# A clustered-attention and two-stage MoE kernel on one core: a reordered prologue, PSUM operands for some VectorE work, and contiguous early-expert weights

## The chip, the cores and the metric

One core of one Trainium2 chip runs the whole program. Its engines are PE (TensorE: matrix products, with the weight loads listed apart as PEld), DVE (VectorE), ACT (ScalarE), POOL (GpSimd) and SP (SyncE, which here only issues DMAs). Each engine runs its own instructions in order; semaphores tie the engines together. SBUF is the working memory of 128 partitions, PSUM the memory that PE writes to, in eight banks. The metric is the device time of one execution in microseconds, as a median of several runs.

## What is computed

Three stages follow each other: attention with a mask from clusters, an MLP with squared ReLU, and a mixture of eight experts with the best expert for each token.

```python
# attention: batch 2, 8 heads, 768 tokens, 64 wide, 16 centroids per head
q_assign = argmax(normed(q) @ normed(centroids).T, -1); k_assign = the same for k
mask = q_assign[:, :, :, None] == k_assign[:, :, None, :]
scores = where(mask, 0.125 * q @ k.T, -1e9)
x = softmax(scores) @ v                      # -> 1536 tokens x 512
# MLP, 512 -> 2048 -> 512 (w_in, w_out come as float64)
h = maximum(x @ w_in, 0);  x = (s * h * h + b) @ w_out
# experts: 8, 512 -> 1024 -> 512
logits = normed(x) @ normed(expert_emb).T / tau
e = argmax(logits); gate = softmax(logits)[e]
out = gate * (maximum(x @ w1[e], 0) @ w2[e])
```

## The kernel before

**Attention** works on 16 heads (2 batches of 8). Its order is written out by hand: `attention` collects (time, step) pairs in `ops`, sorts them, and pins each step's instructions on all five engines in that order. Head j's steps lie at 12 j plus the offsets in `TIMES`; head j's scores begin at 12 j. The steps of a head are these. `load` issues its q, k and v. `split` makes a rounded copy on ACT and the rest on POOL (on DVE for head 0). `trans` transposes one half of q or k by PE into the PSUM bank "t" (four banks for head 0 alone), copies it by ACT and, after the second half, sends it to the score operand by a DMA from SP. `sims_mm` multiplies with the centroids; `sims_a` to `sims_e` find the nearest one on DVE; `masks` transposes the result into the SBUF tile `ot` and copies it into rows 64 to 95 of the operands `qa` and `ka`: for heads 0 and 1 by ACT and DVE, for heads 2 and 3 by four DMAs of 32 rows, later by DMAs of 16. `M` forms one of twelve score blocks and DVE takes its row maxima; `mneg` and `mrow` turn them into a row that a DMA writes into row 96 of `qa`. `Sx` then forms a score block again with mask and maximum inside (L247, L248) and takes the exponential by ACT (L249). `presum` adds exponentials on POOL, `V` multiplies with v, `sums`, `norm_a` to `norm_c` normalise; the PSUM bank "s2" is shared by `sums`, the maximum row and the first head's maxima. `cst.heat` (`HEAT`) issues matmuls of no use that keep PE busy.

Before, the maxima of head j begin 17.4 steps ahead of its scores. The first head's maxima thus lie among the preparations of heads 1 and 2, each with two warming matmuls, and half of head 1's maxima are formed ahead of head 0's scores. `moe.hooks` adds steps of the later stages to this list: constants (`early`, at `SETUP`), fetches of the float64 weights from ACT's queue (`FETCH`), and their conversion to float32 in nine steps per weight (`CONV`, `conv_steps`) for the first five weights (`NWA`).

**The MLP** (`moe1`) runs three chunks of 512 tokens. A weight block f loads or splits its weights (`wsplit`: ACT rounds, POOL subtracts), forms 12 + 12 matmuls and evacuates. The remaining weights are converted in chunk 0 through PSUM. The routing of chunk c (`route`) runs in pieces, one per weight block of chunk c + 1: `locate` compares the index row `iotas` with each token's rank on DVE, `collect` multiplies the resulting 0/1 matrices, and after chunk 1 `pick` chooses an expert for early work. `eweights` loads its weights by indirect DMAs from POOL; `take` gathers 128 of its tokens. The early expert block (`early_block`, handed out by `fill`) then fills PE while the last chunk is routed and the first rows for the experts are gathered. **The experts** (`experts`, `block`) follow, one after another.

The order in the MLP and the experts is left to the scheduler, but for ACT and DVE in the last routing.

Of the kernel before, what the change touches and what calls it, by code (L numbers as in the profile page):

```python
# [21 lines left out]
P = 128  # L22
# [9 lines left out]
             M=-17.4, mneg=-5.7, mrow=-3.5, V=(5.45, 5.45, 9.45, 9.45, 13.45, 13.45), presum=3.0, norm=(14.5, 25.47, 29.5, 29.5, 29.5))  # L32
ENDS = {14: (14.5, 21.47, 22.4, 23.4, 24.4), 15: (14.5, 14.6, 14.7, 14.8, 14.9)}
WARM = -26
HEAT = ((-41, 7), (-30.5, 6), (-22, 6))
SETUP, FETCH = 6.3, (5.3, 17.3, 29.3)
# [57 lines left out]
def attention(ax, tc, cst, q, k, v, cen, xt, hooks, embed):  # L94
# [110 lines left out]
    def masks(j):  # L205
        i = j % NSET
        ot = w1.tile([P, HS], F32, name="ot", tag="ot")
        nc.vector.transpose(out=ot, in_=si.pop(j))
        for g in range(4):
            da, w = (qa, ka)[g // 2][i], slice(g % 2 * HS, (g % 2 + 1) * HS)  # L210
            if j >= NSET:
                nc.sync.dma_start(out=da[64:64 + NC_, w].bitcast(F32), in_=ot[32 * g:32 * g + NC_])
            elif j > 1:
                nc.sync.dma_start(out=da[64:96, w].bitcast(F32), in_=ot[32 * g:32 * g + 32])
            elif g % 2 == 0:
                nc.scalar.activation(out=da[64:96, w], in_=ot[32 * g:32 * g + 32], func=AF.Copy)
            else:
                nc.vector.tensor_copy(da[64:96, w], ot[32 * g:32 * g + 32])

# [127 lines left out]
    T = TIMES  # L347
    for j in range(NH):
        o = 12 * j
        if j >= 3:  # L350
# [8 lines left out]
        for i, f in enumerate((sims_a, sims_b, sims_c, sims_d, sims_e, masks)):  # L359
            at(o + T["simv"][i], f, j)  # L360
        for r in range(NR):
            for c in range(2):
                at(o + T["M"] + 2 * r + c, M, j, r, c)
                if j == 0:
                    at(o + T["M"] + 2 * r + c, cst.heat, 2, "pv")
        at(o + T["mneg"], mneg, j)
        at(o + T["mrow"] if j else -5.6, mrow, j)
# [13 lines left out]
class Moe:  # L381
# [11 lines left out]
    def hooks(self, ms, mb):  # L393
# [11 lines left out]
        out = [(-27, self.length), (SETUP, early), (-16.6, self.unit), (SETUP + 9, self.project)] + [(t, lambda f=f: fetch(f)) for f, t in enumerate(FETCH)]  # L405
        for f in range(NWA):
            for n, t in enumerate(CONV):
                out.append((36 * f + 16 + t if f < NWA - 1 else 176.2 + n, lambda f=f: next(self.steps(f), None)))
        return out

    def steps(self, f):
        if f not in self.running:
            self.running[f] = self.conv_steps(f)
        return self.running[f]

    def conv_steps(self, f, wide=False):
# [3 lines left out]
        u = [self.ps([P, DM], "cv", "ab"[a]).bitcast(U32) if wide else t[:, a] for a in range(2)]  # L420
        for a in range(2):
            nc.scalar.activation(out=t[:, a].bitcast(F32), in_=r[a][:, :, 1].bitcast(F32), func=AF.Abs)
            yield
        s = t.rearrange("p a (w o) -> p o (a w)", o=2)
        nc.vector.tensor_scalar(out=s.bitcast(F32), in0=s.bitcast(F32), scalar1=CLAMP_LO, scalar2=CLAMP_HI, op0=ALU.max, op1=ALU.min)
        yield
        shift = dict(scalar1=5, scalar2=2, op0=ALU.logical_shift_left, op1=ALU.logical_shift_right)
        if wide:
# [766 lines left out]
```

## Time and profile before

| | us |
|---|---|
| median of 3 runs | 801.79 (798.8 to 803.8) |
| profiled execution | 798.36 |
| its span, first to last instruction | 796.5 |
| PE busy | 758.3 |
| DVE busy | 521.5 |
| ACT busy | 422.7 |
| POOL busy | 347.6 |

Attention fills the span up to about 281 us, the MLP up to about 562, the experts the rest. Busy time is what the profile counts for an engine's instructions; matmuls are pipelined, so a busy PE isn't PE at its peak. The granted clock of PE has two levels, 1.2 and 2.4 GHz, given as 0.5 and 1.0; its mean over the span is 0.983.

### The profile page before, as it was taken

To read this page: it belongs to the slowest core of one execution; us is meant where nothing else is said; L and a number is where in the kernel's file an instruction comes from. 1 tells how busy PE (TensorE), PEld (TensorE's weight loads), DVE (VectorE), ACT (ScalarE), POOL (GpSimd) and SP (SyncE) were. 2 spreads that over 40 slices of the span, in tenths; PEclk is the share of its full clock that TensorE was granted. 3 is DMA by queue.
4 is the path that set the end of the run, shared out by engine and by line. 5 is a ranking of instruction groups with operands and counts; after the bars stand their busy time and mean duration, and the time that the engine had idled before them with its cause. 6 is when DMAs were issued, how large, how long until landed. Compare 5 with 4: busy or idle time off the path is not lost. (4 is left out here: it accounts for less than half of the span.)

```text
span 796.5 us, 12226 instructions
## 1 busy us (share of the span) xinstructions
PE 758.3 (95%) x4193; PEld 574.0 (72%) x4193; DVE 521.5 (65%) x1087; ACT 422.7 (53%) x841; POOL 347.6 (44%) x277
## 2 busy tenths in 40 slices
PE   7699999999999899999999999999999999999994
PEld 3365555555555378888788887778889998989883
DVE  5768889897996889984353542647457445756750
ACT  5266555655644576545445554454447455755650
POOL 2066766776686474454344443545032202230000
PEclk9799999999999999999999999999999999999998
DMA  5145433434321225511000042254133664776600
GB/s 151 41 124 175 113 117 80 137 94 129 87 78 50 73 64 159 177 35 54 1 0 1 27 146 92 80 211 146 56 116 121 222 211 138 243 238 209 217 17 24
DMA packets 75469, 88.72 MB, mean 111 GB/s; under 512 B 7445, under 2 KB 58549, under 8 KB 75008
## 3 DMA queue, kind: packets, MB, share of 16 engines
q1 hardware_dynamic: 66688, 66.52, 27.5%
q0 software_dynamic: 4000, 13.90, 5.4%
q10 hardware_dynamic: 4704, 7.34, 2.8%
q8 instruction: 40, 0.66, 0.3%
q14 instruction: 37, 0.30, 0.1%
HBM read 70.57 MB, written 7.34 MB: 98 GB/s over the span
## 5 line engine op out<-in xcount | busy, mean ns | idle before, releaser
L531 POOL TENSOR_TENSOR wl<-w,wh 128x512 fp32r<-128x512 f32 x96 | 123.0, 1306 | 130.9 <-ACT wh L529 128.3
L249 ACT ACTIVATE pt<-S 128x384 f32<-128x384 f32 x192 | 91.8, 489 | 102.9 <-PE S L248 100.4
L224 DVE TENSOR_REDUCE mx<-M 128x1 f32<-128x384 f32 x192 | 101.9, 552 | 37.7 <-PE M L223 35.7
L260 POOL TENSOR_TENSOR acc<-acc,pt 128x768 f32<-128x768 f32 x61 | 106.3, 1742 | 5.7 <-ACT pt L249 3.3
L552 PE MATMUL hp<-x,wh 128*128 128x512 f32 x384 | 105.9, 397 | 0.2 <-ACT wh L529 0.2
L552 PE MATMUL hp<-x,spare 128*128 128x256 f32 x732 | 96.0, 284 | 2.0 <-PEq L987 1.7
L552 PEld LDWEIGHTS hp<-x,spare 128*128 128x128 f32 x732 | 92.6, 190 | 6.9 <-issue 4.1
L560 PE MATMUL y<-wd,gg 128*128 128x512 f32 x360 | 93.2, 394 | 0.0
L608 DVE SCALAR_TENSOR_TENSOR hp<-hp,sb,t 128x512 f32<-128x512 f32 x48 | 36.3, 757 | 74.1 <-ACT t L607 74.1
L552 PEld LDWEIGHTS hp<-x,wh 128*128 128x128 f32 x384 | 71.2, 189 | 15.1 <-ACT wh L529 0.9
L223 PE MATMUL M<-ka,qa 80*128 80x384 f32 x192 | 78.2, 408 | 3.9 <-DVE mx L224 3.1
L560 PE MATMUL y<-wh,gh 128*128 128x512 f32 x192 | 75.0, 391 | 0.0
L560 PE MATMUL y<-wl,gh 128*128 128x512 f32 x192 | 74.8, 389 | 0.0
L268 PE MATMUL pv<-pt,vn 128*64 128x385 f32 x384 | 74.0, 507 | 0.0
L247 PE MATMUL S<-qa,ka 97*128 97x384 f32 x192 | 71.0, 370 | 2.2 <-ACT pt L249 1.4
L545 DVE TENSOR_TENSOR wd<-w,wd 128x512 fp32r<-128x512 f32 x64 | 43.3, 686 | 44.1 <-ACT wd L544 43.4
L560 PEld LDWEIGHTS y<-wd,gg 128*128 128x128 f32 x360 | 63.8, 189 | 9.9
L1036 POOL DMA_INDIRECT row<-rows,idx x24 | 27.9, 1163 | 93.9 <-PE tp L1048 50.8
L607 ACT ACTIVATE t<-hp 128x512 f32<-128x512 f32 x48 | 28.7, 598 | 71.7 <-PE hp L552 71.7
L248 PE MATMUL S<-qb,kb 128*128 128x384 f32 x192 | 65.5, 341 | 0.0
L223 PEld LDWEIGHTS M<-ka,qa 80*128 80x128 f32 x192 | 36.7, 191 | 38.0 <-DVE su L296 8.1
L560 PE MATMUL y<-wh,gl 128*128 128x512 f32 x192 | 59.1, 389 | 0.0
(269 smaller groups left out, 1361.2 us busy)
## 6 DMA issues: line engine op xcount, KB each, us to landing
w<-in_moe_w_dram SPq DMA_DIRECT2D x128, 256.0 KB
raw<-in_moe_w_in_dram SPq DMA_DIRECT2D x9, 512.0 KB
raw<-in_moe_w_out_dram SPq DMA_DIRECT2D x9, 512.0 KB
raw<-in_moe_w_in_dram ACTq DMA_DIRECT2D x7, 512.0 KB
raw<-in_moe_w_out_dram ACTq DMA_DIRECT2D x7, 512.0 KB
qn<-in_q_dram SPq DMA_DIRECT2D x16, 192.0 KB
kn<-in_k_dram SPq DMA_DIRECT2D x16, 192.0 KB
vn<-in_v_dram SPq DMA_DIRECT2D x16, 192.0 KB
```

Source lines behind the costliest of these rows:

```text
L223: nc.tensor.matmul(pp, qa[i][0:80, r * P:(r + 1) * P], ka[i][0:80, c * HS:(c + 1) * HS])
L224: nc.vector.tensor_reduce(out=mxt[j % 2][:, r, c:c + 1], in_=pp, axis=AX.X, op=ALU.max)
L247: nc.tensor.matmul(pp, ka[i][0:97, t * P:(t + 1) * P], qa[i][0:97, w], start=True, stop=False)
L248: nc.tensor.matmul(pp, kb[i][:, t * P:(t + 1) * P], qb[i][:, w], start=False, stop=True)
L249: exps.setdefault((j, t), []).append(nc.scalar.activation(out=p[:, c, 0:HS], in_=pp, func=AF.Exp, scale=0.125).ins)
L260: eng.tensor_tensor(out=acc[j][-1], in0=acc[j][-1], in1=p[:, :, 0:HS], op=ALU.add)
L268: together(tc, [lambda c=c: nc.tensor.matmul(pv_t[j][c * 64:c * 64 + 64, :], io_t["v", j][:, t, :], p[:, c, :], start=t == 0, stop=t == NR ...
L531: eng.tensor_tensor(out=wl[:, a], in0=w[:, a], in1=wh[:, a].bitcast(F32), op=ALU.subtract)
L545: eng.tensor_tensor(out=t[:, 1], in0=w[:, a], in1=t[:, 0].bitcast(F32), op=ALU.subtract)
L552: self.nc.tensor.matmul(hp, a[:, k * P:(k + 1) * P], b(k), start=n == 0, stop=n == 3 * KD - 1)
L560: self.nc.tensor.matmul(y[i], (gl if n == 2 else gh)[:, s], wl if n == 1 else wh, start=first and n == 0, stop=last and n == 2)
L608: nc.vector.scalar_tensor_tensor(out=hp, in0=hp, scalar=sb[:, 0:1], in1=t, op0=ALU.mult, op1=ALU.mult)
```

## The change

The times of the attention steps get a table for heads 0 to 4 (`FIRST`) in place of `TIMES`. Head 0's maxima come straight behind its masks, 0.4 steps apart and with one warming matmul each, its maximum row right behind them; the warming groups ahead and behind are 16 and 10 long. Heads 2 and 3 are transposed and given their masks later, behind the first scores of head 0; the maxima of heads 1, 2 and 3 come later and closer together. Heads 0 to 2 transpose their masks inside PSUM (`ot` is the PSUM tile itself) and copy them from there, half by DVE in `masks`, half by ACT in the new step `copies`; head 2 issues no mask DMAs any more. The constants move ahead of the first scores, the weight fetches and the conversion steps of weights 0 to 3 move back by 6 and 12 steps. Weight 4 is converted through the PSUM banks M0 and M1. In `route`, the last third of the index row is copied to PSUM for chunks 0 and 1 and compared from there, the first two thirds are compared in plain order, and a factor of the gates is copied to PSUM. The early expert's second weights come in eight indirect DMAs of 128 rows of 2 KB instead of three, with hidden units in their own order, so that its first weights are read in contiguous columns.

```diff
@@ -29,11 +29,16 @@
 MASK = float(2 ** 33)
 GUARD = 1e-9
 TIMES = dict(load=-49, loadv=-18, split=(-42, -40), trans=(-36.6, -35.6, -33.6, -32.6), sims=-30.53, simv=(-26.5, -26.5, -26.5, -22.52, -22.52, -22.51),
-             M=-17.4, mneg=-5.7, mrow=-3.5, V=(5.45, 5.45, 9.45, 9.45, 13.45, 13.45), presum=3.0, norm=(14.5, 25.47, 29.5, 29.5, 29.5))
+             M=(-17.4, 1), mneg=-5.7, mrow=-3.5, V=(5.45, 5.45, 9.45, 9.45, 13.45, 13.45), presum=3.0, norm=(14.5, 25.47, 29.5, 29.5, 29.5))
 ENDS = {14: (14.5, 21.47, 22.4, 23.4, 24.4), 15: (14.5, 14.6, 14.7, 14.8, 14.9)}
 WARM = -26
-HEAT = ((-41, 7), (-30.5, 6), (-22, 6))
-SETUP, FETCH = 6.3, (5.3, 17.3, 29.3)
+FIRST = {0: dict(TIMES, M=(-22.4, 0.4), mneg=-17.85, mrow=-17.8),
+         1: dict(TIMES, trans=(-36.6, -34.2, -33.4, -32.6), sims=-31.5, simv=(-29.5, -29.5, -29.5, -29.4, -29.4, -29.3), copies=-11.5, M=(-9.9, 0.5), mneg=-4.2, mrow=-3.8),
+         2: dict(TIMES, split=(-42, -41.5), trans=(-23.6, -22.6, -21.4, -20.6), sims=-18.53, simv=(-16, -16, -16, -16, -16, -15.9), copies=-12.6, M=(-12.4, 0.75), mneg=-3.9),
+         3: dict(TIMES, load=-66, split=(-33, -31), trans=(-29.4, -28.4, -27.4, -25.6), sims=-22.53, simv=(-21.9, -21.1, -20.3, -19.5, -19.4, -18.7), M=(-14.4, 0.8), mneg=-4.8),
+         4: dict(TIMES, sims=-26.53, simv=(-25.5, -25.5, -25.5, -22.52, -22.52, -22.51))}
+HEAT = ((-41, 7), (-30.5, 16), (-17.7, 10))
+SETUP, FETCH = -16.5, (11.2, 23.2, 35.2)
 CONV = (3.2, 5.2, 7.2, 11.2, 15.2, 19.2, 23.2, 27.2, 31.2)
 F, DM, TC = 2048, 512, 512
 NF, KD, NTT = F // P, DM // P, TC // P
@@ -204,18 +209,21 @@
 
     def masks(j):
         i = j % NSET
-        ot = w1.tile([P, HS], F32, name="ot", tag="ot")
-        nc.vector.transpose(out=ot, in_=si.pop(j))
+        pp = si.pop(j)
+        ot = sm[j] = w1.tile([P, HS], F32, name="ot", tag="ot") if j > 2 else pp
+        nc.vector.transpose(out=ot, in_=pp)
         for g in range(4):
             da, w = (qa, ka)[g // 2][i], slice(g % 2 * HS, (g % 2 + 1) * HS)
             if j >= NSET:
                 nc.sync.dma_start(out=da[64:64 + NC_, w].bitcast(F32), in_=ot[32 * g:32 * g + NC_])
-            elif j > 1:
+            elif j > 2:
                 nc.sync.dma_start(out=da[64:96, w].bitcast(F32), in_=ot[32 * g:32 * g + 32])
-            elif g % 2 == 0:
-                nc.scalar.activation(out=da[64:96, w], in_=ot[32 * g:32 * g + 32], func=AF.Copy)
-            else:
+            elif g % 2:
                 nc.vector.tensor_copy(da[64:96, w], ot[32 * g:32 * g + 32])
+
+    def copies(j):
+        for g in (0, 2):
+            nc.scalar.activation(out=(qa, ka)[g // 2][j % NSET][64:96, 0:HS], in_=sm[j][32 * g:32 * g + 32], func=AF.Copy)
 
     def M(j, r, c):
         i = j % NSET
@@ -344,9 +352,9 @@
     at(-30, lambda: [nc.sync.dma_start(out=ka_[96:97, :].bitcast(F32), in_=one) for ka_ in ka])
     for t, f in hooks:
         at(t, f)
-    T = TIMES
     for j in range(NH):
         o = 12 * j
+        T = FIRST.get(j, TIMES)
         if j >= 3:
             at(o + T["load"], load, j, "qk")
             at(o + T["loadv"], load, j, "v")
@@ -358,13 +366,16 @@
         at(o + T["sims"], sims_mm, j)
         for i, f in enumerate((sims_a, sims_b, sims_c, sims_d, sims_e, masks)):
             at(o + T["simv"][i], f, j)
+        if j < 3:
+            at(o + T.get("copies", T["simv"][5]), copies, j)
         for r in range(NR):
             for c in range(2):
-                at(o + T["M"] + 2 * r + c, M, j, r, c)
+                first, step = T["M"]
+                at(o + first + step * (2 * r + c), M, j, r, c)
                 if j == 0:
-                    at(o + T["M"] + 2 * r + c, cst.heat, 2, "pv")
+                    at(o + first + step * (2 * r + c), cst.heat, 1, "pv")
         at(o + T["mneg"], mneg, j)
-        at(o + T["mrow"] if j else -5.6, mrow, j)
+        at(o + T["mrow"], mrow, j)
         for t in range(NR):
             for c in range(2):
                 at(o + 2 * t + c, Sx, j, t, c)
@@ -402,32 +413,35 @@
             self.loaded[f] = self.load_f64(f, nc.scalar)
 
         self.loaded, self.wT, self.wraw, self.running = {}, {}, {}, {}
-        out = [(-27, self.length), (SETUP, early), (-16.6, self.unit), (SETUP + 9, self.project)] + [(t, lambda f=f: fetch(f)) for f, t in enumerate(FETCH)]
+        out = [(-27, self.length), (SETUP, early), (-16.6, self.unit), (20.3, self.project)] + [(t, lambda f=f: fetch(f)) for f, t in enumerate(FETCH)]
         for f in range(NWA):
             for n, t in enumerate(CONV):
-                out.append((36 * f + 16 + t if f < NWA - 1 else 176.2 + n, lambda f=f: next(self.steps(f), None)))
+                out.append((36 * f + 28 + t if f < NWA - 1 else 176.2 + n, lambda f=f: next(self.steps(f), None)))
         return out
 
     def steps(self, f):
         if f not in self.running:
-            self.running[f] = self.conv_steps(f)
+            self.running[f] = self.conv_steps(f, ("M0", "M1") if f == NWA - 1 else None)
         return self.running[f]
 
-    def conv_steps(self, f, wide=False):
+    def conv_steps(self, f, banks=None):
         nc = self.nc
         r = self.loaded.pop(f)
         t = self.w32(f, U32)
-        u = [self.ps([P, DM], "cv", "ab"[a]).bitcast(U32) if wide else t[:, a] for a in range(2)]
+        u = [self.ps([P, DM], "cv", b).bitcast(U32) for b in banks] if banks else [t[:, 0], t[:, 1]]
+        early = banks is not None and f < NWA
+        z = u if early else [t[:, 0], t[:, 1]]
         for a in range(2):
-            nc.scalar.activation(out=t[:, a].bitcast(F32), in_=r[a][:, :, 1].bitcast(F32), func=AF.Abs)
+            nc.scalar.activation(out=z[a].bitcast(F32), in_=r[a][:, :, 1].bitcast(F32), func=AF.Abs)
             yield
         s = t.rearrange("p a (w o) -> p o (a w)", o=2)
-        nc.vector.tensor_scalar(out=s.bitcast(F32), in0=s.bitcast(F32), scalar1=CLAMP_LO, scalar2=CLAMP_HI, op0=ALU.max, op1=ALU.min)
+        for y in z if early else (s,):
+            nc.vector.tensor_scalar(out=y.bitcast(F32), in0=y.bitcast(F32), scalar1=CLAMP_LO, scalar2=CLAMP_HI, op0=ALU.max, op1=ALU.min)
         yield
         shift = dict(scalar1=5, scalar2=2, op0=ALU.logical_shift_left, op1=ALU.logical_shift_right)
-        if wide:
+        if banks:
             for a in range(2):
-                nc.vector.tensor_scalar(out=u[a], in0=t[:, a], **shift)
+                nc.vector.tensor_scalar(out=u[a], in0=z[a], **shift)
         else:
             nc.vector.tensor_scalar(out=s, in0=s, **shift)
         yield
@@ -562,7 +576,7 @@
     def convert(self, f):
         if f in self.wT:
             return
-        for _ in self.running.get(f) or self.conv_steps(f, True):
+        for _ in self.running.get(f) or self.conv_steps(f, "ab"):
             pass
 
     def after(self, *ins):
@@ -685,8 +699,8 @@
         for i, t in enumerate(lt):
             copy(i, part[:, i * each:(i + 1) * each], t)
         yield
-        rt = self.ps([P, 3, n, 32], "rt", "M0" if final else "b")
-        lg, nb, gt = rt[:, 0, :, 0:E], rt[:, 1, :, 0:8], rt[:, 2, :, 0:4]
+        rt = self.ps([P, 4, n, 32], "rt", "M0" if final else "b")
+        lg, nb, gt, last = rt[:, 0, :, 0:E], rt[:, 1, :, 0:8], rt[:, 2, :, 0:4], rt[:, 3].rearrange("p n w -> p (n w)")
         for i in range(n):
             nc.tensor.matmul(lg[:, i], part[:, i], self.fold)
         fill(0)
@@ -697,6 +711,8 @@
         nc.vector.tensor_reduce(out=m[:, :, 0:1], in_=lg, axis=AX.X, op=ALU.max)
         nc.vector.tensor_tensor(out=w, in0=lg, in1=bc(m[:, :, 0:1]), op=ALU.is_equal)
         nc.scalar.activation(out=l, in_=lg, func=AF.Copy)
+        if not final:
+            nc.scalar.activation(out=last, in_=self.iotas[:, 2 * P:3 * P], func=AF.Copy)
         if final:
             for i in range(n):
                 square(i)
@@ -719,10 +735,7 @@
 
         def locate(j0, j1):
             for i in range(n):
-                o, s = [t[:, j0 * P:j1 * P] for t in (ohr[i], self.iotas)]
-                if not final:
-                    o, s = [t.rearrange("p (w o) -> p o w", o=2) for t in (o, s)]
-                nc.vector.tensor_scalar(out=o, in0=s, scalar1=self.rank[:, g0 + i:g0 + i + 1], scalar2=None, op0=ALU.is_equal)
+                nc.vector.tensor_scalar(out=ohr[i][:, j0 * P:j1 * P], in0=last if j0 and not final else self.iotas[:, j0 * P:j1 * P], scalar1=self.rank[:, g0 + i:g0 + i + 1], scalar2=None, op0=ALU.is_equal)
 
         def collect(j0, j1, v0, v1, tag):
             si = self.ps([P, j1 - j0, v1 - v0, E], "si", tag)
@@ -775,7 +788,8 @@
         for z in range(3):
             nc.vector.tensor_copy(gb[:, :, z:z + 1], gt[:, :, z:z + 1])
             nc.vector.tensor_tensor(out=gt[:, :, z + 1:z + 2], in0=gt[:, :, z:z + 1], in1=gb[:, :, z:z + 1], op=ALU.subtract)
-            nc.vector.tensor_tensor(out=v[:, :, 2 + z], in0=oh, in1=bc(gb[:, :, z:z + 1]), op=ALU.mult)
+            nc.vector.tensor_copy(nb[:, :, 4 + z:5 + z], gb[:, :, z:z + 1])
+            nc.vector.tensor_tensor(out=v[:, :, 2 + z], in0=oh, in1=bc(nb[:, :, 4 + z:5 + z]), op=ALU.mult)
         yield
         collect(0, 3, 2, 5, "y0" if final else "a")
         if c == NT // TC - 2:
@@ -811,20 +825,17 @@
         self.eup = [up[k // 2][:, k % 2] for k in range(KD)]
         self.edown = [down[0][:, f] if f < 4 else down[f // 2 - 1][:, f % 2] for f in range(NF2)]
         self.eload = []
-        for tiles, src, each in ((up, self.w1, KD), (down, self.w2, NF2)):
-            r0 = 0
+        for n, tiles, src, each, step in ((0, [t.rearrange("p r w -> p (r w)") for t in up], self.w1.rearrange("e (q r) w -> (e q) (r w)", r=2), KD // 2, 1), (2, self.edown, self.w2.rearrange("e q w -> (e q) w"), 1, P)):
+            r = sm.tile([P, len(tiles)], U32, name="wr", tag=f"wr{n}", bufs=1)
+            nc.vector.scalar_tensor_tensor(out=s[:, 6:7], in0=s[:, 4:5], scalar=float(src.shape[0] // E // each), in1=self.iotap, op0=ALU.mult, op1=ALU.add)
             for i, t in enumerate(tiles):
-                n = t.shape[1]
-                r = sm.tile([P, 1], U32, name="wr", tag=f"wr{each}{i}", bufs=1)
-                nc.vector.scalar_tensor_tensor(out=r, in0=s[:, 4:5], scalar=float(P), in1=self.iotap, op0=ALU.mult, op1=ALU.add)
-                nc.vector.tensor_scalar(out=r, in0=r, scalar1=float(each // n), scalar2=float(r0 // n), op0=ALU.mult, op1=ALU.add)
-                self.eload.append((t, src.rearrange("e (q r) w -> (e q) (r w)", r=n), r))
-                r0 += n
+                nc.vector.tensor_scalar(out=r[:, i:i + 1], in0=s[:, 6:7], scalar1=float(each), scalar2=float(i * step), op0=ALU.mult, op1=ALU.add)
+                self.eload.append((t, src, r[:, i:i + 1]))
 
     def eweights(self):
-        if self.eload:
+        for _ in range(min(len(self.eload), 1 + len(self.eload) % 2)):
             t, src, r = self.eload.pop(0)
-            self.nc.gpsimd.indirect_dma_start(out=t.rearrange("p r w -> p (r w)"), out_offset=None, in_=src, in_offset=bass.IndirectOffsetOnAxis(ap=r, axis=0), bounds_check=src.shape[0] - 1, oob_is_err=False)
+            self.nc.gpsimd.indirect_dma_start(out=t, out_offset=None, in_=src, in_offset=bass.IndirectOffsetOnAxis(ap=r, axis=0), bounds_check=src.shape[0] - 1, oob_is_err=False)
 
     def take(self):
         nc, sm, m, m0 = self.nc, self.sm, self.m, self.m0
@@ -870,7 +881,7 @@
         for f in range(NF2):
             hp = self.ps([P, P], "hpe", ("M1", "y1")[f % 2])
             for k in range(KD):
-                nc.tensor.matmul(hp, self.eup[k].rearrange("p (i f) -> p f i", f=NF2)[:, f], x[:, k], start=k == 0, stop=k == KD - 1)
+                nc.tensor.matmul(hp, self.eup[k][:, f * P:(f + 1) * P], x[:, k], start=k == 0, stop=k == KD - 1)
             nc.scalar.activation(out=g[f // 4][:, f % 4], in_=hp, func=AF.Relu)
             yield
         y = self.ps([P, DM], "ye", "y2")
```

## Rows read from the trace of the kernel before

**Rows 1.** The page, part 1: busy us, share of the span, instructions.

```profile
PE 758.3 (95%) x4193; PEld 574.0 (72%) x4193; DVE 521.5 (65%) x1087; ACT 422.7 (53%) x841; POOL 347.6 (44%) x277
```

**Rows 2.** Windows: length, busy us by engine (instructions), clock, DMA share, GB/s.

```profile
34.90:41.50 6.60, 4.93 (x20) 4.47 (x20) 5.14 (x13) 2.01 (x5) 0.00 (x0) 0.50 0.25 75
...
277.20:281.90 4.70, 4.52 (x17) 1.54 (x16) 3.11 (x7) 2.46 (x6) 0.00 (x0) 0.64 0.21 50
519.31:523.20 3.89, 3.89 (x13) 2.77 (x13) 2.36 (x24) 0.51 (x1) 0.80 (x1) 0.56 0.42 135
```

**Rows 3.** Timeline: start us, us, engine, line, output<-input, count [idle before <-releaser].

```profile
9.16 2.36 PE L1133 MATMUL heat<-work 128*128 128x512 bf16 x6
...
31.88 0.56 DVE L224 TENSOR_REDUCE mx<-M 128x1 f32<-128x384 f32 x1 [2.18 <-PE M L223]
...
33.25 0.81 SPq L238 DMA_DIRECT2D qa<-mrs  x1
...
38.08 0.52 PE L247 MATMUL S<-qa,ka 97*128 97x384 f32 x1
...
97.76 0.34 PE L247 MATMUL S<-qa,ka 97*128 97x384 f32 x1
...
260.46 0.73 SPq L238 DMA_DIRECT2D qa<-mrs  x1
...
262.38 0.41 PE L247 MATMUL S<-qa,ka 97*128 97x384 f32 x1 [0.45 <-DMA qa<-mrs]
```

**Rows 4.** Timeline of PE's weight loads in head 1's scores.

```profile
65.88 0.19 PEld L223 LDWEIGHTS M<-ka,qa 80*128 80x128 f32 x1
...
66.41 0.41 PEld L162 LDWEIGHTS tp<-identr,ks 128*128 128x128 f32 x3
```

**Rows 5.** Groups by line, attention: count | busy us, mean ns | idle before.

```profile
L224 DVE TENSOR_REDUCE mx<-M 128x1 f32<-128x384 f32 x192 | 101.9, 552 | 37.7 <-PE M L223 35.7
L249 ACT ACTIVATE pt<-S 128x384 f32<-128x384 f32 x192 | 91.8, 489 | 102.9 <-PE S L248 100.4 <-PE mr L235 0.9 <-PE M L223 0.3
```

**Rows 6.** Conversion: groups; single lines (ns min/median/max, starts); the wait behind it.

```profile
L425 DVE TENSOR_SCALAR w<-w 128x1024 f32<-128x1024 f32 x5 | 9.1, 1820 | 3.0 <-ACT w L422 3.0
...
L432 DVE TENSOR_SCALAR w<-w x5: 685/686/2077, 72.6 to 263.2; 128x1024 uint32<-128x1024 uint32 x5
...
L437 DVE SCALAR_TENSOR_TENSOR w<-raw,cv x22: 672/677/683, 291.4 to 353.0; 128x512 uint32<-128x512 uint32 x22
L437 DVE SCALAR_TENSOR_TENSOR w<-raw,w x10: 679/1249/2318, 82.6 to 267.9; 128x512 uint32<-128x512 uint32 x10
...
275.55 0.87 PE L284 MATMUL su<-acc,ones 128*64 128x384 f32 x4 [2.25 <-DVE xu L303]
```

**Rows 7.** Timeline of locating in chunks 0 and 1; the waits of PE.

```profile
421.61 0.89 DVE L725 TENSOR_SCALAR ohr<-iotas,rank 128x128 bf16<-128x128 f16 x4
...
515.14 3.91 DVE L725 TENSOR_SCALAR ohr<-iotas,rank 128x128 bf16<-128x128 f16 x4
...
PE si L731 <- DVE ohr L725: 2.5, 3, 1.0
```

**Rows 8.** Timeline of early and later block; a wait (us, times, longest).

```profile
575.59 1.01 POOL L1036 DMA_INDIRECT row<-rows,idx  x1 [22.16 <-DVE ohr L725]
...
576.16 3.89 PEld L873 LDWEIGHTS hpe<-x,eup 128*128 128x128 f32 x16
...
583.75 1.03 PEld L1048 LDWEIGHTS tp<-ident,row 128*128 128x128 f32 x8
...
633.56 1.98 PEld L1075 LDWEIGHTS hp<-x,w 128*128 128x128 f32 x16
...
DVE ntok L895 <- PE cn L894: 3.2, 1, 3.2
```

**Rows 9.** POOL: the early loads by line; the weight split by group.

```profile
L827 POOL DMA_INDIRECT edn<-in_moe_w_dram,wr x3: 990/1003/1005, 525.2 to 537.6; - x3
...
L531 POOL TENSOR_TENSOR wl<-w,wh 128x512 fp32r<-128x512 f32 x96 | 123.0, 1306 | 130.9 <-ACT wh L529 128.3
```

## What the change was predicted to do

> **What bounds the kernel now.** I read the page first, then windows of equal length, then the waits, and last the timeline of the four places where these showed lost time or dear work. The page gives TensorE (PE) 758 of 796.5 us busy [rows 1], so a microsecond is won only where PE waits, runs at its lower clock, or does work that can be made cheaper. The chain that the page follows back says little here: most of it is DMA that other work covers. There are four such places, three of them seen in windows of the clock [rows 2]. From 34.9 to 41.5 the granted clock is 0.50, the 1.2 GHz level, after PE has waited for its first heads; at the end of attention PE runs at 0.64 of its clock from 277.2 to 281.9, right behind a wait of 2.25 us [rows 6]; at 519.3 to 523.2 it runs at 0.56. The fourth, the early expert block after 564, has no gap: PE is full, but with slow weight loads. Behind it the experts keep PE full to the end, so what is won earlier stays won.
>
> **The prologue (A).** Before, the first score matmul starts at 38.08 and head 4's at 97.76 [rows 3], 59.7 us for four heads, part of it at half clock. The change puts head 0's twelve maxima straight behind its masks. I walk the new order. The warming matmuls start at 9.16; six took 2.36 us there, half that each once the clock is up, so sixteen end near 13.6. PE, ScalarE (ACT), VectorE (DVE), GpSimd (POOL) and SP each run their own part of the list in order, so the two mask copies on ACT stand behind head 1's first transposed copy: three transposes, 0.41 of weight loads [rows 4] and their latency, to 14.1, then three ACT passes of 0.49 (an exponential of that shape, [rows 5]), to 15.6. DVE is through head 0's masks by then. Twelve maxima of 0.55 [rows 5] would end at 22.8 if DVE were the limit; PE also does nine transposes, twelve warming matmuls and head 1's similarities between them, and I take 24.0. From the end of the last maximum (31.88 + 0.56) to the issue of the row DMA it was 0.8, and from such an issue to the score matmul that waits for it 1.9 [rows 3]. So head 0's scores start at 26.7 instead of 38.1: 11.4 earlier.
>
> Not all of it is won. Moved behind that point are head 2's four transposed halves and one of head 3's (5 x 0.41), head 2's similarities (0.8, estimated from their four 384-column matmuls) and six of head 1's maxima matmuls (0.18 each: M and a pair of scores take 0.53 from 65.88 to 66.41 [rows 4]): 4.0 us of PE work. The half clock goes: half of the 3.4 us behind 38.08, 1.7 back. Then stalls. In head 0's twelve steps ACT now holds 12 exponentials, 9 transposed copies, 4 mask copies (heads 1 and 2), 4 splits and the row copy: 30 passes of 0.49 are 14.7 us, where PE needs some 15. The transposes share one PSUM bank, so PE and ACT hand it back and forth. By the walk PE loses 2.5 us at the start (head 1's mask copies stand between two exponentials, and head 1's maxima wait for them) and 1.5 at the end (head 2's similarities come on DVE only behind head 1's twelve maxima, and head 2's copies and maxima behind those); half a microsecond each for casts that read PSUM instead of SBUF lies beside these. Heads 1 to 3 repay the rest: one head's similarities and five maxima matmuls, already in the 4.0. I book 5 us as lost to stalls (the walk's 4 and one for what it misses): 11.4 - 4.0 + 1.7 - 5 = **4.1**. Bounds: 9.1 without stalls, 0 if they double. Head 3's earlier load costs SP two issues while it waits for nothing; the setup constants now run on DVE and POOL before head 0's scores, small instructions in DVE's queue ahead of head 1's maxima and inside the 2.5. Moving the weight fetches and conversions twelve steps later I cost at nothing: conversion 3 still ends before the last one starts, and PE's own work hides DVE's in those heads; if it didn't, one weight's passes on DVE, 8.3 us as counted under B, would be what heads 1 to 3 save and heads 11 to 13 repay.
>
> **The last early weight conversion (B).** For weight 4, clamp, shift and merge go through PSUM banks M0 and M1, free behind head 15's maxima. Before, clamp took 1.82, shift up to 2.08, the second merge up to 2.32 while POOL was adding; the same merge with one input in PSUM took 0.67 to 0.68, never more, with POOL as busy [rows 6]. Eight passes at 0.68 are 5.4 against 1.82 + 2.08 + 3 x 0.68 + 2.32 = 8.3: 2.8 saved on DVE. Head 13's normalisation stands behind these in DVE's queue, and PE waits 2.25 for it [rows 6]. That wait goes (2.2 of it), and of the low clock behind it, 4.7 x 0.36 = 1.7 [rows 2], I take half, since ACT is late there too: **3.0**, bounds 1 and 3.9. Late next is the exponential of head 15, which PE feeds itself.
>
> The Trainium skill, VectorE: DVE Perf Modes, section Why PSUM operands drop a tier, speaks against this: a PSUM operand keeps fp32 at one element per cycle. The trace agrees on the price (the shift of 1024 elements took 0.69 when undisturbed, and 512 from PSUM cost as much [rows 6]); by the rule alone B would lose 1.4 us, by the rows of the contended case it saves 2.8.
>
> **Locating tokens (C).** In chunk 1's routing four comparisons take 3.91 us beside POOL's weight split and PE waits 2.5 us for them; undisturbed, four took 0.89 in chunk 0 [rows 7]. They now read a PSUM copy of the index row (one more ACT pass, off the path). The wait goes, and the 0.56 clock right behind it (3.89 x 0.44 = 1.7 [rows 2]): **4.2**, bounds 2.5 and 4.3. The first two thirds stay in SBUF and may still wait for POOL, but PE uses them only a whole weight block later.
>
> **The early expert block (D).** Its up weights are now contiguous columns instead of every eighth element. Sixteen loads took 3.89 us with the stride and 1.98 for contiguous weights of the same shape in a later block [rows 8]: 64 loads save 4 x 1.91 = 7.6 us. PE is full there, and the routing stands behind those loads: DVE alone waits 3.2 us for the matmul of the counts. But POOL gathers the expert's rows behind the indices, at 575.59, and PE loads them for transposing at 583.75 [rows 8]; about half of the loads stand ahead of that gather, so it comes some 3.8 earlier while PE arrives 7.6 earlier; a part of the 8.2 us between the two is cover, and I expect PE to wait some 2 for the rows. The extra copies to PSUM add three small passes before the gates, 0.2 on the path as an estimate. I take **5.4**, bounds 3 and 7.6.
>
> **The ten indirect loads (E).** Five more POOL issues, 1.0 each, spread as 1, 2, 2, 2, 2, 1 over six weight blocks. POOL's two split passes take 2.6 of a block [rows 9], and 48 blocks between 281.9 and 576 [rows 2, 8] are at most 6.1 each, so two issues fit beside them: 0.1 us.
>
> Sum: 4.1 + 3.0 + 4.2 + 5.4 - 0.1 = 16.6. The profiled execution took 798.4, so it becomes 781.8; the median of the runs, 801.8, lies 3.4 above, and becomes **785.2**.
>
> **Rivals.** (1) The prologue gives nothing: ACT, as full as PE in head 0, stalls PE 9 us or more and the earlier start is paid back. For it: the ACT count above; against it: heads 1 to 3 have less DVE work than before, as the conversions left. 785.2 + 4.1 = 789.3. (2) The early block only filled time: the routing chain and the gather set its length. For it: ACT, not PE, carries squares, a table load and the exponential there; against it: DVE's waits on PE. D falls to 1: 789.6. (3) The load time does not hang on the stride, so D is 0: 790.6. For it no row speaks. The Trainium skill, TensorE: Matmul & The Clock Gate, section LDWEIGHTS (loading the stationary operand), says that columns alone set it; the trace differs, sixteen loads of 128 columns took 3.89 us strided and 1.98 contiguous [rows 8]. (4) The change doesn't do what it says: DVE waits for POOL from PSUM too, and B and C fall away: 792.4. Against it is the merge row with PSUM [rows 6]. (5) Slower: POOL is overrun by the indirect loads. Split passes leave POOL 3.5 of a block of 6.1. If 128 rows of a smaller size held POOL 3.5 us per load, two loads would make the splits late by 3.4 us in each of five blocks and eat the 17: from there it decides; at 4.5 us a load it is 27 lost, 812. Against it: 0.99 to 1.01 us for each of those before [rows 9].
>
> **Numbers.** Chances: forecast 0.62, (1) 0.15, (2) 0.10, (3) 0.02, (4) 0.05, (5) 0.06. The forecast's own bounds: 7.2 more with A and D at their upper ends gives 778, the upper ends of B and C and the scatter of the runs 776. Upwards the range takes in rivals 1 to 4 and their scatter: 793. A difference under 1% (8 us, bound 793.8) can't be told from no change. Faster holds the forecast and rivals 1 to 3, with a little of (4): 0.90; same takes the rest of (4) and a mild (5): 0.07; slower 0.03.
>
> **What would show it.** A: first score matmul near 26.7, head 4's near 93.5, clock 1.00 there. B: no gap before head 14's sums. C: locating under 1.2 us for four and no PE wait on it. D: sixteen loads in about 2 us, and the gathered rows transposed some 17 us earlier than 583.75. E: no wait of PE for POOL's weight splits in chunk 2. Wrong would be head 4's scores later than 97, or PE waiting over 5 us for gathered rows.

## The result, and the profile after

The changed kernel takes 791.25 us (median of 6 runs, 789.8 to 792.93) against 799.06 (798.42 to 803.8): ratio 0.9889, 95% interval 0.9861 to 0.9916. The forecast was 785.2, with a range of 776 to 793. So the side and the range hold, but of 16.6 us only about 8 came: 5.4 in the two profiled executions (span 791.1 against 796.5). That the time lies within 6 us of the forecast is in part luck: the kernel before took 799.06 in these six runs, 2.7 us less than the 801.79 that the forecast started from. The markers on TensorE (PE) say where the gain came and where it was lost, in us:

| stretch | before | after | difference | forecast |
|---|---|---|---|---|
| start to head 0's scores | 38.08 | 25.67 | -12.4 | -11.4 |
| head 0's scores to head 4's | 59.68 | 77.20 | +17.5 | +7.3 |
| head 4's to head 15's | 164.62 | 165.63 | +1.0 | 0 |
| head 15's to the first MLP matmul | 19.54 | 17.24 | -2.3 | -3.0 |
| to the first matmul of the early block | 282.70 | 279.06 | -3.6 | -4.1 |
| to the first expert | 25.70 | 19.21 | -6.5 | -5.4 |
| to the end | 206.18 | 207.09 | +0.9 | 0 |

All of B, C and D came, 12.4 us of 12.5. The prologue, A, was to win 4.1 and lost 6.1. Head 4's scores start 5.1 us later than in [rows 3].

Windows of the kernel after, head 0's scores to head 4's, head by head and in one (length, busy us of each engine, then TensorE's granted clock, DMA share, GB/s):

```profile
25.67:48.86 23.19, 18.66 (x89) 11.09 (x90) 14.96 (x47) 12.99 (x30) 13.34 (x14) 0.84 0.27 68
48.86:67.97 19.11, 18.52 (x97) 10.51 (x96) 10.53 (x25) 8.15 (x20) 7.24 (x6) 0.84 0.40 118
67.97:87.09 19.12, 17.49 (x91) 10.05 (x90) 15.10 (x35) 10.02 (x24) 9.65 (x7) 0.91 0.36 105
87.09:102.87 15.78, 15.11 (x86) 9.06 (x86) 13.75 (x29) 8.71 (x22) 10.50 (x8) 1.00 0.57 164
25.67:102.87 77.20, 69.78 (x358) 40.71 (x358) 54.34 (x134) 39.88 (x95) 40.72 (x33) 0.89 0.39 109
```

The same stretch of the kernel before:

```profile
38.08:97.76 59.68, 58.28 (x330) 36.81 (x330) 48.11 (x113) 34.56 (x83) 39.83 (x32) 0.97 0.47 131
```

PE waits 77.20 - 69.78 = 7.4 us where it waited 1.4, and a clock of 0.89 over 77.20 us costs 8.5 where 0.97 cost 1.8. So the 17.5 us are 6.0 of waits, 6.7 of clock, and the rest, 4.8, is work moved behind head 0's first scores.

The timeline of PE after shows how the two hang together (start, us, output<-input, count, [idle before <-releaser]):

```profile
28.89 0.62 PE L231 MATMUL M<-ka,qa 80*128 80x384 f32 x2 [0.76 <-ACT ka L226]
...
31.62 0.52 PE L255 MATMUL S<-qa,ka 97*128 97x384 f32 x1
...
34.05 2.83 PE L276 MATMUL pv<-pt,vn 128*64 128x385 f32 x8
...
42.70 1.51 PE L276 MATMUL pv<-pt,vn 128*64 128x385 f32 x8
...
48.38 0.69 PE L231 MATMUL M<-ka,qa 80*128 80x384 f32 x1 [2.13 <-ACT ka L226]
...
51.38 2.84 PE L276 MATMUL pv<-pt,vn 128*64 128x385 f32 x8
```

Behind a stretch of waits the pv matmuls of a head take 2.83 us where they take 1.51 elsewhere: the granted clock there is 0.50, the 1.2 GHz level. It holds from 31 to 38, from 48 to 55 and from 72 to 75. The waits themselves:

```profile
PE M L231 <- ACT ka L226: 2.9, 2, 2.1
PE tp L167 <- ACT kb L173: 1.6, 4, 0.6
PE M L231 <- DVE mx L232: 1.1, 2, 0.8
```

The three other parts, in the timelines of after: the sums of heads 14 and 15 (B), the four locates (C), and the early block (D).

```profile
279.78 0.87 PE L292 MATMUL su<-acc,ones 128*64 128x384 f32 x4 [0.36 <-DVE xu L311]
...
283.82 1.64 PE L292 MATMUL su<-acc,ones 128*64 128x384 f32 x8 [0.74 <-DVE xu L311]
...
518.96 1.12 DVE L738 TENSOR_SCALAR ohr<-rt,rank 128x128 bf16<-128x128 f32 x4
...
571.83 1.00 POOL L1047 DMA_INDIRECT row<-rows,idx  x1 [17.28 <-DVE ohr L738]
...
572.87 1.86 PEld L884 LDWEIGHTS hpe<-x,eup 128*128 128x128 f32 x16 [0.41 <-ACT ge L885]
...
577.66 0.66 PE L1059 MATMUL tp<-ident,row 128*128 128x128 f32 x4 [0.41 <-DMA row<-rows,idx]
...
583.71 0.45 PE L744 MATMUL si<-vals,ohr 128*128 128x24 bf16 x12 [0.23 <-DVE vals L792]
```

The 2.25 us of [rows 6] are 0.36 and 0.74; the 3.91 us of [rows 7] are 1.12; the 3.89 us of sixteen loads in [rows 8] are 1.86.

### The profile page after: what moved, and what is told of

Read it like the earlier page. It is cut to its first block, busy times and chain, and to the rows that moved or that the text cites. A ratio compares the mean times of both kernels' runs of the same rounds, so it can differ in the third digit from the quotient of the medians.

```text
span 791.1 us, 12255 instructions
## 1 busy us (share of the span) xinstructions
PE 753.7 (95%) x4195; PEld 565.1 (71%) x4195; DVE 522.3 (66%) x1102; ACT 424.6 (54%) x845; POOL 351.6 (44%) x282
## 5 line engine op out<-in xcount | busy, mean ns | idle before, releaser
L276 PE MATMUL pv<-pt,vn 128*64 128x385 f32 x384 | 76.0, 518 | 0.0
L543 ACT ACTIVATE wh<-w 128x1024 fp32r<-128x1024 f32 x48 | 50.4, 1055 | 17.1 <-PE y L574 12.8
```

The source lines that it names most:

```text
L276: together(tc, [lambda c=c: nc.tensor.matmul(pv_t[j][c * 64:c * 64 + 64, :], io_t["v", j][:, t, :], p[:, c, :], start=t == 0, stop=t == NR ...
L543: nc.scalar.activation(out=wh, in_=w, func=AF.Copy)
```

## The experiments

The markers are those of the table. The kernels were measured in three groups of four, each group together with the kernel before, whose median was 800.11, 798.36 and 798.24 us; ratios are to the median of the same group.

**The old prologue, and the new one alone.** The first kernel is after with `FIRST = {0: dict(TIMES, mrow=-5.6)}`, the old warming matmuls, masks, setup and conversion times; the second is before with the new ones.

> The kernel after with the prologue of the kernel before: the order and times of heads 0 to 4, the masks, the warming matmuls, the setup and the weight conversions 0 to 3 are put back; the last early conversion, the locating, the early expert block and its loads stay as changed. Theory: the new prologue is what ate the gain. By the traces head 4 starts 5.1 us later than before and head 15 6.1 us later, so without it 791.25 - 6.1 = 785 us (783 to 787), and first scores near 38, head 4's near 97.8. Rival: the prologue is worth the 4.1 us that I forecast and the late heads are a matter of that one profiled execution: 795 us.

> The kernel before with the new prologue alone (first maxima early, heads 1 to 4 later, masks from PSUM, setup and conversions moved). Theory: slower by what heads 1 to 4 lost, 799.1 + 6 = 805 us (803 to 807), first scores near 25.7 and head 4's near 102.9. Rival: the parts work against one another (the conversions, moved by twelve steps, collide with the last early one only in the kernel after), and the prologue alone brings its 4.1: 795 us.

Measured: 789.13 us (0.9865, 0.9814 to 0.9915), and 803.98 (1.006, 1.0033 to 1.0087). Alone, the new prologue makes the kernel slower: head 4's scores come at 100.4 instead of 97.8. The first kernel fell between its theories. Its head 15 started at 260.1, 8.4 us earlier than in after (262.4 and 6.1 in a later execution, below), but from the early block's first matmul to the first expert it took 21.80 us instead of 19.21, with a new wait of 3.2 us for the gate values. The same program ran again later:

> The same program as the first run with the old prologue (789.1 us), on another chip. Three programs of that call had ScalarE's last two relus 3.7 us late in the early block, and two executions of the kernel after, profiled elsewhere, had not. If the late relus belong to the program, the wait of 3.2 us for the gate values and the half clock behind it are here again: 789 us, and 21.8 us from the block's first matmul to the first expert. If they belonged to that chip or that moment, they are gone: 19.2 us for the stretch and 784.5 us.

It took 790.81 us (0.9911, 0.989 to 0.9933), with that wait again. In its timeline ScalarE's (ACT) last two relus and GpSimd's (POOL) seventh gather, and what waits behind them on PE:

```profile
568.87 0.28 ACT L876 ACTIVATE ge<-hpe 128x128 f32<-128x128 f32 x1 [0.62 <-issue]
571.47 0.28 ACT L876 ACTIVATE ge<-hpe 128x128 f32<-128x128 f32 x1 [2.33 <-PE tp L1050]
574.46 0.28 ACT L876 ACTIVATE ge<-hpe 128x128 f32<-128x128 f32 x1 [2.71 <-PE ye L880]
...
574.75 1.00 POOL L1038 DMA_INDIRECT row<-rows,idx  x1 [1.49 <-PE ye L880]
...
580.19 0.45 PE L735 MATMUL si<-vals,ohr 128*128 128x24 bf16 x12 [2.73 <-DVE vals L783]
```

The window behind it, of 20 us, with the clock at 0.91, 1.8 us more:

```profile
580.49:600.49 20.00, 20.00 (x139) 18.83 (x136) 14.52 (x32) 11.82 (x25) 3.32 (x3) 0.91 0.14 44
```

So 2.7 + 1.8 = 4.5 us of the old prologue's gain went into the early block. The late relus came again on a second chip, so they go with the program.

**Holding the clock in the stalls.** After, with 28 warming matmuls where PE waited:

```
+    for t, n in ((0.45, 1), (2.05, 4), (2.59, 2), (8.15, 2), (11.39, 2), (11.55, 10), (24.39, 3), (24.79, 4)):
+        at(t, cst.heat, n, "s2")
```

> The kernel after with 28 more warming matmuls at the places where TensorE waited in heads 0 and 1 (in front of the second key transpose of head 2, of head 1's and head 2's first maxima, and in head 1's last steps), writing a PSUM bank that is free there. Theory: the three stretches at half clock behind those waits (31 to 38, 48 to 55 and 72 to 75 us) cost the most; with TensorE busy in the gaps the granted clock stays at 1.00 from 25 to 103 us and head 4 starts 6 to 8 us earlier than 102.9: 791.25 - 7 = 784 us (783 to 787). Rival: ScalarE and VectorE set the pace of these heads, the half clock only fills their waits, and the warming matmuls stand in the way: 790 to 793 us.

791.16 us (0.9879, 0.9831 to 0.9928): no gain at the end, and yet the theory of the clock held where it speaks. From head 0's scores to head 4's it took 69.99 us instead of 77.20, and head 15 started 6.3 us earlier; then the early block took 21.78 us (a wait of 3.3) and a half clock behind it took 2.6 more.

**Masks through SBUF.** `ot = sm[j] = w1.tile(...)` for all heads.

> The kernel after, but heads 0 to 2 have their transposed masks written to SBUF, as heads 3 and up have, and copied from there. Theory: in PSUM ScalarE's two mask copies wait until VectorE's two are through (2.1 us for the four where 1.05 did before); with SBUF the first maximum of head 0 starts some 1.1 us earlier than 15.34 and head 1's 1.1 us earlier, so 1 to 2.5 us less: 789.5 us. Rival: the copies from SBUF wait for GpSimd's subtractions as the long strided operations did, and nothing is gained: 791 us.

793.95 us (0.9893, 0.9861 to 0.9925), with the late relus too. Head 0's first maximum came at 15.48, no earlier: its mask copies on ACT stand behind head 1's first transposed copy in both kernels (in after that ends at 14.30, when the two of VectorE, DVE, have ended at 14.16). Head 1's first maximum came 2.66 us behind head 0's scores instead of 3.22. But head 2's two copies on DVE took far longer from SBUF, beside POOL's adding, so the rival held for that head. Below them stand the same two from PSUM, in after, where POOL was adding as well:

```profile
46.19 1.83 DVE L222 CAST qa<-ot 32x384 fp32r<-32x384 f32 x1
48.04 1.74 DVE L222 CAST ka<-ot 32x384 fp32r<-32x384 f32 x1
```

```profile
45.31 0.55 DVE L222 CAST qa<-si 32x384 fp32r<-32x384 f32 x1
45.87 0.56 DVE L222 CAST ka<-si 32x384 fp32r<-32x384 f32 x1
```

The time can't show the half microsecond of head 1.

**After again, and the gate chain first.** The second kernel takes the scaling, the exponential and the gate values of the last routing ahead of the counts, the last relus and the row copies:

```
+        if final:
+            scale()
+            nc.scalar.activation(out=l, in_=l, func=AF.Exp)
             self.counts()
...
-        for _ in range(2):
+        for _ in range(3):
             next(self.stages)
         prep(0)
```

> The kernel after once more, on the chip of the next three. Its first profile had TensorE waiting 0.2 us for the gate values at the end of the early expert block; three kernels with the same block waited 2.8 to 3.3 us there, behind ScalarE's last two relus, which came 3.7 us late, and ran at half clock behind it. Theory: that wait belongs to the new block and the first profile of after escaped it by chance; now it shows, with 21.8 us from the block's first matmul to the first expert instead of 19.2, and the time is as before, near 791 us. Rival: the wait came with what those three kernels changed in the prologue: 19.2 us again.

> The kernel after, with one change of order in the last routing: the gate chain (scaling, exponential, gate values) is taken ahead of the counts, of the last two relus and of the copies of the gathered rows on ScalarE and VectorE. Theory: the wait for the gate values and the half clock behind it go, since 3 us of VectorE work no longer stand behind ScalarE's late relus; the stretch from the block's first matmul to the first expert falls to some 18.7 us, and the time to 791 - 4 = 787 us where the wait had been there, 790.5 where it had not. Rival: the late relus hold the exponential as well, or the row copies become the last to come: the stretch stays near 21.8 and the time at 791 us.

790.5 us (0.9896, 0.9858 to 0.9934), with 19.21 for the early stretch: the theory fell, after does not have the late relus. And 790.08 us (0.9896, 0.9859 to 0.9934), with 18.97: nothing to gain where they are not late. But no kernel with the gate chain first had the wait, so it serves as a base for what follows. The stretch from head 0's scores to head 4's in these two, after again and the base:

```profile
25.80:100.01 74.21, 66.55 (x357) 39.27 (x358) 54.23 (x134) 39.70 (x95) 40.71 (x33) 0.93 0.40 113
```

```profile
24.92:102.09 77.17, 69.71 (x357) 40.72 (x358) 54.35 (x134) 39.87 (x95) 40.70 (x33) 0.89 0.38 109
```

PE's waits are 7.7 and 7.5 us, as in the first profile of after (7.4). The clock is not the same: one and the same program loses 8.5 us to it in one execution and 5.2 in the other.

**The prologue and the clock, each alone, on that base.**

> The kernel after with the gate chain first and the old prologue, nothing else: it differs from the kernel with the gate chain first (790.1 us) by the prologue alone, and the wait of the early block can't blur the comparison. Theory: the new prologue costs 5 to 6 us as it stands, so 784.5 us (783 to 786.5). Rival: in most executions the two prologues are worth the same, and the first profiles were a chance: 789 to 790 us.

> The kernel after with the gate chain first and the 28 warming matmuls in the stalls of heads 0 and 1, nothing else: against 790.1 us it shows what the half clock alone costs. Theory: 6 to 7 us, as head 4 started 6.4 us earlier with them in the first such run, so 783.5 us. Rival: that gain was given back later in that run for a reason of its own kind, and is again: 788 to 790 us.

786.29 us (0.986, 0.9841 to 0.988) and 785.3 (0.9844, 0.9826 to 0.9863) against 790.08, the base in the group before. So the new prologue costs 3.8 us as it stands; with the clock held it is 4.8 us faster and then 1.0 ahead of the old one. The stretch from head 0's scores to head 4's of the warmed kernel:

```profile
26.32:96.36 70.04, 67.78 (x383) 39.82 (x386) 54.25 (x134) 39.74 (x95) 40.69 (x33) 1.00 0.43 120
```

**The strided weights again, on that base.**

> The kernel after with the gate chain first, and the early block's weights loaded and laid out as before (every eighth column, six loads of twice the size). Theory: 64 weight loads of 243 ns instead of 124 (16 took 3.89 us strided, 2 us contiguous) make the stretch from the block's first matmul to the first expert 18.97 + 6.5 to 7.6, near 26 us, and the time 790.1 + 6.5 = 796.6 us. Rival: with the gate chain first the stretch has slack and less of the 7.6 us is seen: 793 us.

796.29 us (0.9981, 0.9963 to 0.9999): 6.2 us slower than with contiguous weights. The stretch took 25.70 us, as before, and its loads

```profile
575.50 3.89 PEld L894 LDWEIGHTS hpe<-x,eup 128*128 128x128 f32 x16
```

The chunks ahead of it took 278.26 us, 0.8 less than after: that is what ten early loads cost instead of five, where I had said 0.1. Half of it lies in one weight block among the loads (from 535.97 in after: 5.84 us against 5.44), half behind 553.1, when they are over.

**Both prologues, tuned.** The new one with the 28 warming matmuls, 9 more around head 0's maxima, SBUF masks, and head 0's mask copies ahead of head 1's first transposed copy; the old one with warming matmuls alone. Both with the gate chain first.

> The kernel after with everything learnt for its new prologue: the warming matmuls in the stalls (28 there, 8 more in front of head 0's first maximum), the masks of heads 0 to 2 through SBUF, head 0's mask copies ahead of head 1's first transposed copy on ScalarE, and the gate chain first. Theory: first scores near 24.5 us (25.7 before), 69 us from head 0's scores to head 4's instead of 77.2, so head 15 near 259.5 instead of 268.5, and the end 9 + 2 us earlier than after: 780 to 782 us. Rival: what is saved in the prologue comes back as waits in heads 2 to 4, head 15 stays near 262 and the time near 786 us.

> The kernel after with the prologue of before, to which only warming matmuls are added (6 at the start, 14 where TensorE waits for head 2's last query copy, 17 between the last maxima of head 0 and the first scores), and the gate chain first. Theory: head 0's scores start at 35 us at half clock no more, head 0 takes 12.4 us instead of 13.95, head 15 comes near 257.5 to 258.5; with the gate chain 5 us less than the 789.1 of the old prologue with the other parts, and 1.5 to 2 for the clock: 782 to 783 us. If this and the tuned new prologue come out alike, the early maxima as such are worth nothing and the clock was all; rival: the new prologue, freed of its half clock, is 2 us or more ahead.

784.02 us (0.9817, 0.9779 to 0.9854; runs from 782.8 to 784.9) and 786.24 (0.9846, 0.9806 to 0.9886; 784.7 to 787.8). The new one beats before and after, though head 2's two copies on DVE, from SBUF again, take 1.82 and 1.75 us. Each missed its forecast by 2 to 4 us. The old one kept its clock at 1.00 and won nothing by it: 786.24 us against 786.29 without the warming matmuls, and head 0 took 14.01 us where it had taken 13.94 to 14.99:

```profile
46.65 0.42 PE L224 MATMUL M<-ka,qa 80*128 80x384 f32 x1 [1.25 <-DMA ka<-ot]
```

At full clock PE waits for head 2's masks instead. With the warming matmuls on both sides the new prologue is 2.2 us ahead.

## Why the prediction was right in its side and wrong in its size

**A failed, at one step.** The order of the prologue was walked well: head 0's scores at 25.67 (forecast 26.7), the moved work 4.8 (4.0), the stalls 6.0 (5.0 booked). The step that failed is "The half clock goes: half of the 3.4 us behind 38.08, 1.7 back". I had counted the stalls as time lost once, and put the clock at 1.00 over them. They cost twice: 8.5 us at half clock in after (5.2 in its second execution) where before lost 1.8, so +6.7 where I had -1.7. That is 8.4 us of the 9.2 by which head 4 missed; 1.0 of stalls and 0.8 of moved work, less 1.0 of an earlier start, make the rest. The warming matmuls show that it is the clock: with it at 1.00 the stretch takes 70.04 us against 77.17 in its base, though PE does more work, and the time falls by 4.8 us. Of the 67.78 us that PE is busy there, 6.99 are warming matmuls; the 60.8 left are close to what 69.71 us come to without 8.5 of half clock. The Trainium skill, TensorE: Matmul & The Clock Gate, section HAM oscillation — how this bites in real kernels, describes a kernel whose PE waits for DMA behind each short piece of work, longer than the piece takes, and whose clock drops each time. The trace agrees that it drops again and again, 0.84, 0.84 and 0.91 in heads 0 to 2, but it does so behind shorter waits, of at most 2.13 us, most of them for ACT. It would have been the rival to weigh. What I named as wrong, "head 4's scores later than 97", came: 102.9. Rival (1) had the direction and a part of the reason: some 5 of the 7.4 us of waits are for ACT, where it had 9 or more. It left out the clock, and stopped at nothing gained.

A smaller cost that I put at nothing: the conversions moved by twelve steps. Heads 4 to 15 take 1.0 us longer, 165.6 to 165.7 us in all kernels with the new times and 164.6 to 164.7 with the old; most of it in head 13's steps, 13.76 instead of 13.01. There two merges of 2.08 and 1.77 us now stand between the maxima on DVE, and PE waits 1.6 us for maxima in the last 50 us ahead of head 15's scores, where it waits 0.5 with the old times. No run moved the conversions alone.

Masks in PSUM were also costed as an engine's half microsecond. In after ACT's copies of head 1 start at 27.87, when DVE's two casts end, and the four passes take 2.14 us; from SBUF, in the kernel before, head 1's ran side by side in 1.05. The Trainium skill, PSUM — Partial Sum Buffer, section PSUM bank collisions raise a hardware error, forbids two engines at once only within the same 32 partitions of a bank. These four copies each read 32 partitions of their own, and the program waits all the same: the trace shows a stricter order than the page asks for. Against this stands what PSUM spared head 2, as the kernel with SBUF masks shows: 3.57 us for its two copies on DVE instead of 1.11.

**B was right,** 2.3 us of 3.0: the eight passes are 0.67 to 0.70 each, as costed, and what is left is 1.1 us of waits of head 14's and 15's sums for the normalisation of heads 13 and 14. On DVE it still stands behind two passes of 2.27 and 2.09 us, beside POOL's adding, where such a pass takes 0.68 otherwise.

**C was right,** 4.4 of 4.2 (282.70 to 278.26, from the kernel with the strided weights), by 1.12 us for four locates and no wait of PE. **E** was 0.8 instead of 0.1. Rival (5) is out all the same: the eight loads of the second weights held POOL 1.00 to 1.02 us each. Its price was added up wrongly too: spread as 1, 2, 2, 2, 2, 1, two loads stand in four blocks, not five, some 14 us and not 17.

**D was right,** 6.5 of 5.4, and 6.7 with the gate chain first. With the block's first matmul at 564.6 before and 564.8 after, the gather is issued 3.8 us earlier (575.59 in [rows 8], 571.83), as walked, and PE waits 0.4 us for its rows instead of the 2 that I had taken off. With B, C and D come, rivals (2) and (4) are out. Rival (3) is out: with all else equal sixteen loads take 3.89 us strided and 1.86 contiguous. The Trainium skill, in the section LDWEIGHTS (loading the stationary operand) of the page named above, has columns alone set the time; the measurement decides against it for these weights of 32-byte steps.

**What stays open.** Why three programs with the new block (four executions) have ACT's last two relus late, the first by 1.6 to 3.1 us and the second by 3.7: by the profile they wait for PE alone, whose matmuls had ended, and POOL's seventh gather is late with them. The one with SBUF masks has the same order on PE, ACT and POOL as after, which has them in time. Nor is it known why the end, behind the last matmul, is some 0.7 us longer in all kernels with contiguous weights (11.8 to 12.1 instead of 11.2 to 11.3 us).

## What to carry to other kernels

When work is reordered so that PE starts earlier but waits more, book each stall twice: once as the wait, and once as the half clock that may follow it; the first can hide behind the earlier start, the second does not. Where a stall can't be removed, warming matmuls that write a free PSUM bank take the second half back (7 us of the stretch and 4.8 of the time here), but only where PE is what the others wait for; in the old prologue they won nothing. A change of several parts is best read by markers on the bounding engine: each part had its own stretch here, and three of four forecasts held to about a microsecond while the sum was off by half.

## What the runs showed of the hardware that was not expected

The clock of one and the same program differs between executions. With the old prologue the first scores came at 35.76 us in one and at 38.09 in the other, on another chip. About 1 us of the difference is there by the first maximum (15.76 and 16.75): from 8 to 10 us the granted clock was 1.00 in the one and 0.50 in the other. In the stretch from 28 to 32, behind 24 to 28 where PE was busy for 1.5 and 0.6 us, the granted clock was 1.00 in the first and 0.57 in the second:

```profile
28.00:32.00 4.00, 2.83 (x16) 1.02 (x15) 2.21 (x5) 0.79 (x3) 1.60 (x2) 1.00 0.22 49
```

```profile
28.00:32.00 4.00, 4.00 (x16) 1.11 (x16) 1.21 (x3) 0.87 (x2) 0.99 (x1) 0.57 0.22 49
```

Much of the scatter of the kernel before (796 to 804 us) may lie there; no trace of a long run was taken, but in the three groups its eight runs above 801.5 us have mean clocks of 0.977 to 0.979, and all its others 0.981 or more. The kernel with the tuned new prologue, whose mean clock is 0.992 to 0.996, took 782.8 to 784.9 us.
